# Soft-MoE after soft-capped attention: the last two batches' slot sums on VectorE instead of TensorE, and one filler product less per batch

## The chip, the cores and the metric

The kernel runs on one core of a Trainium2 chip. The metric is the device time of one execution in microseconds (us). Before the change it was 288.38 us, the median of three runs (287.92 to 288.79).

## The reference

Attention over 8 batches, 12 heads, 448 tokens and a head width of 64, with scores capped by tanh, feeds a mixture of experts with soft slots: 3584 tokens of width 768, 8 experts with 4 slots each, so 32 slots.

```
scores = 30 * tanh(q @ k.T / 8 / 30)
attn   = exp(scores - max); attn /= attn.sum(-1)
x      = attn @ v, heads side by side            # 3584 x 768

logits = x @ phi                                 # 3584 x 32
d      = exp(logits); d /= d.sum(0)              # over the tokens
h      = relu((d.T @ x)[e] @ w1[e])              # for each expert e, its 4 slots
slot_out[e] = h @ w2[e]
c      = exp(logits); c /= c.sum(1)              # over the 32 slots of a token
out    = c @ slot_out                            # 3584 x 768
```

The change is about the last softmax: the sum over the 32 slots of each token, by which that token's row of the output is divided.

## The kernel before

All engines' work is issued in one order written out by hand; a list `aux` says which extra job goes into which slot of which step.

**Attention.** A pair is two heads of one batch, with the pair's 448 tokens in 7 tiles of 64 for each head. The 336 tiles are worked off in 56 chunks of six (`CH = 6`), and a batch takes seven chunks (`PER`). In chunk j, ACT takes the tanh of two lots of three score tiles (`tanh_chunk`, L329) and the exponentials of chunk j-1 (`exp_part`, L334), of which DVE does some by a polynomial (L564 to L572). PE forms the scores of the next chunk (`qk_chunk`, L320) into one of two PSUM homes, and the products of the exponentials with V (`pv_mms`, L590). POOL casts V (L287) and issues most of the loads. Each chunk has slots e, a, b, r, c, d, and in slot a of some chunks stand fillers: products of ones into the unused 57 columns of the home of `pv` (`fill`, L620), whose results nobody reads. `FILL` lists them by chunk: (7, 'a', fill, 24) is 24 fillers in slot a of each batch's eighth chunk, between the V products of the first four tiles (`pv_first`) and those of the last 64 query rows (`pv_tail`), ahead of the next `qk_chunk`. It is so in seven batches; for the eighth there is no such chunk.

**Logits, E and the slot inputs.** For each batch PE forms the logits (`logits`, 128 tokens by 32 slots in four groups of tokens, NG = 4, the fourth with 64 rows per half), ACT their exponential `es[b]`, called E (L677, for the last batch L960), and PE the sums E.T @ x (`slot_mms`) over all batches. E has tokens on the partitions and the 32 slots along the free dimension. For the output it is needed turned, with slots on the partitions (`e_transp`): `ET4` for the first six batches, `ETl` for the last two. Batches go in twos: tile c of the batches 2bb and 2bb+1 is one product of 128 tokens.

**The sums.** `e_sums(bb)` (L702 to L706) takes, for one couple of batches, seven products of the turned E with a column of ones (L705) and the reciprocal of the seven sums (L706) into `winv[:, bb, :]`. For the first three couples that stands in the attention part; for the fourth, in the last loop, in front of tile n = 19.

**The tail.** After the last chunk, the last batch's logits and slot sums, then layer 1 of all experts (L1018), relu on ACT and DVE (L1025, L1027), `h_transp` (turns h, L1035, copied by L1039), and layer 2 in two halves of 384 columns (L1046): `for n0 in range(0, 64, 4)` with `layer2(n0, 0)`, then again with half 1. In the first of these loops, at n0 = 16, `h_transp(1)` and `widen(B - 2)` (L1061, DVE: four copies of E side by side, so that one product turns and widens it) are issued. `zdiag`, a float32 tile of 128 x 4 x 32, is used once before that, for the token sums of d (L982, L984).

**Output.** While half 1 of layer 2 runs, the first halves of tiles 0 to 11 are formed (`half_tile`: product L1086, scaling by `winv` on DVE L1088 or ACT L1090, store L1074). Then a loop over n = 0 to 27 forms the second halves of those (n < 12) and both halves of the others (product L1133, scaling L1140 on DVE for odd n, L1142 on ACT for even n). In it, at n = 15 and 17 `e_transp` turns E of the last two batches (L692, L696), and at n = 19 `e_sums(3)` follows. Tiles 21 to 27 are those of the last couple and read `ETl` and `winv[:, 3, :]`. The 11.0 MB of output are stored by SP's queue (L1074), which also reads the spilled part of w2 back before that (L997). The buffers of the output tiles are shared in turn, so a scaling can wait for an earlier store to land.

## Time and profile before

| what | value |
|---|---|
| median of three runs | 288.38 us |
| the profiled execution | 288.24 us |
| its span, first to last instruction | 286.5 us |
| PE busy, products | 250.3 us (87%), 4706 |
| DVE busy | 242.6 us (85%), 502 |
| ACT busy | 254.6 us (89%), 211 |
| POOL busy | 138.9 us (48%), 197 |
| mean granted TensorE clock | 0.981 |
| DMA | 68.11 MB, mean 238 GB/s |

The profile is of one execution; its busy times are shares of a span in which attention, until about 241 us, and the tail have different limits. "Busy" of an engine is time with an instruction on it, so a share near 100% in a stretch says that the engine had no time left there, and the averages over the span do not. In the lists of the timeline, a bracket gives the idle time of that engine before the instruction, and what ended it. PE's weight loads have rows of their own (PEld). A line like L590 is a line of the kernel before.

### The profile page before, as it was taken

How to read it: one execution, taken by the hardware profiler on the slowest of the kernel's cores; microseconds unless marked ns; L12 is line 12 of the kernel's file. 1: busy time of each engine (PE TensorE's matmuls, PEld its weight loads, DVE VectorE, ACT ScalarE, POOL GpSimd, SP SyncE). 2: the span in 40 equal slices, each digit the busy share in tenths (PEclk: the TensorE clock that was granted, in tenths of full speed). 3: DMA queues.
4: the chain of work that ended last, by engine and by line, in shares of the span. 5: the costliest groups of instructions: out<-in, count | busy, mean ns of one | idle time of the engine just before them, and what ended most of it. 6: DMA issues, size and time to landing. Idle time of an engine off the chain costs nothing.

```text
span 286.5 us, 10763 instructions
## 1 busy us (share of the span) xinstructions
PE 250.3 (87%) x4706; PEld 170.3 (59%) x4706; DVE 242.6 (85%) x502; ACT 254.6 (89%) x211; POOL 138.9 (48%) x197
## 2 busy tenths in 40 slices
PE   8888889998999899989998999899899999998710
PEld 7555466756675666566656675667565767642400
DVE  3498999999999999999999999999999986437830
ACT  4999999999999999999999999999999997247720
POOL 7982655664765566555756646574563120200000
PEclk9999999999999999999999999999999999999975
DMA  7999999999999999999999999999999567989995
GB/s 241 257 205 205 201 194 204 224 205 206 232 230 196 209 232 225 217 206 231 227 216 198 226 224 211 214 226 222 206 182 226 137 247 223 409 326 392 414 420 244
DMA packets 58334, 68.11 MB, mean 238 GB/s; under 512 B 4144, under 2 KB 54448, under 8 KB 58288
## 3 DMA queue, kind: packets, MB, share of 16 engines
q0 software_dynamic: 42448, 35.31, 79.1%
q1 hardware_dynamic: 15552, 31.89, 31.7%
q8 instruction: 37, 0.61, 0.8%
q10 hardware_dynamic: 288, 0.23, 0.2%
q14 instruction: 9, 0.07, 0.1%
HBM read 91.72 MB, written 19.27 MB: 387 GB/s over the span
## 4 chain that ended last, share of the span: by engine, by line
DVE 40%; PE 33%; issue 10%; ACT 8%; POOL 5%; DMA 1%; DVEq 0%; ACTq 0%; SPq 0%
PE pv L590 9%; DVE xq L600 7%; PE sc L320 5%; DVE xp L570 4%; DVE xT L652 4%; DVE ex L571 4%; ACT ex L329 4%; DVE xp L568 3%; ACT ex L334 3%; DVE qT L279 3%; POOL vbd L287 2%; DVE ex L564 2%; DVE xp L569 2%; PE so_ps L1046 2%; DVE xf L566 2%
## 5 line engine op out<-in xcount | busy, mean ns | idle before, releaser
L329 ACT ACTIVATE ex<-sc 128x1344 f16<-128x1344 f32 (+1 forms) x113 | 148.3, 1428 | 1.4 <-PE sc L320 1.4
L334 ACT ACTIVATE ex<-ex 128x2688 bf16<-128x2688 f16 (+5 forms) x58 | 115.1, 1993 | 0.1
L590 PE MATMUL pv<-vbd,ex 128*128 128x130 bf16 (+1 forms) x1610 | 95.0, 211 | 11.4 <-POOL vbd L287 8.5
L590 PEld LDWEIGHTS <-ex 128*128 128x128 bf16 (+1 forms) x1680 | 75.7, 101 | 35.9 <-PE sc L320 9.0
L320 PE MATMUL sc<-qT,kT 64*64 64x448 bf16 x672 | 71.4, 360 | 0.5 <-DVE qT L279 0.4
L287 POOL CAST vbd<-vraw 64x896 bf16<-64x896 f32 x46 | 45.9, 998 | 49.5 <-issue 24.5
L600 DVE TENSOR_TENSOR xq<-pv,rec 128x448 bf16<-128x448 f32 x46 | 28.7, 625 | 1.6
L320 PEld LDWEIGHTS <-kT 64*64 64x64 bf16 x672 | 24.1, 105 | 6.3 <-issue 4.0
L295 POOL MEMSET vbd<- 64x1 bf16 x22 | 3.6, 165 | 45.7 <-PE pv L590 45.7
L570 DVE TENSOR_TENSOR xp<-xp,xf 128x1344 f16<-128x1344 f16 (+2 forms) x34 | 25.1, 738 | 0.8
L568 DVE TENSOR_TENSOR xp<-xp,xf 128x1344 f16<-128x1344 f16 (+2 forms) x34 | 25.0, 736 | 0.6
L116 POOL DMA_DIRECT2D w1b<-in_moe_w_dram x32 | 25.3, 792 | 0.0
L571 DVE TENSOR_TENSOR ex<-ex,xp 128x1344 uint16<-128x1344 uint16 (+2 forms) x34 | 24.7, 727 | 0.4
L567 DVE TENSOR_SCALAR xp<-xf 128x1344 f16<-128x1344 uint16 (+2 forms) x34 | 16.8, 494 | 0.4
L184 POOL DMA_DIRECT2D qb<-in_q_dram x22 | 16.7, 757 | 0.5 <-DMA kraw<-in_k_dram 0.5
L279 DVE COPY kT<-kps 128x896 bf16<-128x896 bf16 x23 | 14.2, 617 | 3.0 <-PE kps L274 2.8
L572 DVE TENSOR_SCALAR ex<-ex 128x1344 uint16<-128x1344 uint16 (+2 forms) x34 | 16.5, 485 | 0.1
L277 PEld LDWEIGHTS <-qb 128*64 128x64 bf16 x308 | 10.1, 109 | 10.9 <-issue 10.9
L184 POOL DMA_DIRECT2D kb<-in_k_dram x22 | 16.2, 735 | 0.1
L569 DVE TENSOR_SCALAR xp<-xp 128x1344 f16<-128x1344 f16 (+2 forms) x34 | 15.7, 462 | 0.6
L120 POOL DMA_DIRECT2D w2d<-in_moe_w_dram x21 | 15.9, 777 | 0.4 <-issue 0.4
L620 PE MATMUL pv<-ones 128*128 128x57 bf16 x376 | 16.0, 188 | 0.0
(124 smaller groups left out, 342.1 us busy)
## 6 DMA issues: line engine op xcount, KB each, us to landing
w1b<-in_moe_w_dram POOLq DMA_DIRECT2D x32, 384.0 KB, 9.1
vraw<-in_v_dram SPq DMA_DIRECT2D x44, 224.0 KB, 6.0
w2d<-in_moe_w_dram POOLq DMA_DIRECT2D x21, 384.0 KB, 8.1
w2t<-w2d SPq DMA_DIRECT2D x21, 384.0 KB, 7.1
out_dram<-ob SPq DMA_DIRECT2D x7, 768.0 KB, 8.2
qb<-in_q_dram POOLq DMA_DIRECT2D x22, 224.0 KB, 7.6
kb<-in_k_dram POOLq DMA_DIRECT2D x22, 224.0 KB, 6.1
w2b<-in_moe_w_dram POOLq DMA_DIRECT2D x11, 384.0 KB, 8.1
```

The costliest lines, as they stand in the source:

```text
L116: pool.dma_start(out=w1b[e][:, js, fs], in_=w1r[:, e, js, fs])
L184: pool.dma_start(out=t, in_=quad_ap(nm, Q))
L279: dve.tensor_copy(t, ps)
L287: pool.tensor_copy(vbds[Q % 2][r, :, :, c0:c0 + DH], raw[r])
L320: pe.matmul(sc[cs, u, 0:S], qkT["k", Q][r, c, cs], qkT["q", Q][r, :, cs], start=True, stop=True)
L329: act.activation(exs[j][:, half * CS + u0:half * CS + u1, :].bitcast(F16), (own[0] if i == u0 == 0 else sc)[:, u0:u1, 0:S], ACT.Tanh, scal ...
L334: act.activation(exs[j][:, u0:u1, :], exs[j][:, u0:u1, :].bitcast(F16), ACT.Exp, scale=cap)
L568: lambda: dve.tensor_tensor(p, p, f, op=ALU.mult),
L570: lambda: dve.tensor_tensor(p, p, f, op=ALU.mult),
L571: lambda: dve.tensor_tensor(y, y, p, op=ALU.add),
L590: pe.matmul(out_, exs[j][r, u, q0:q0 + (HP if tail else P)], v_, start=(c == 0 and g == gs[0] < NF), stop=(c == NT - 1), skip_group_check= ...
L600: dve.tensor_tensor(xq[Q][:, h, s0:s1, :], pv[:, 0:s1 - s0, 0:DH], rec.to_broadcast([P, s1 - s0, DH]), op=ALU.mult)
```

## The change

A new function `e_recips(b)` sums E over the 32 slots with one reduction on VectorE, straight from the tokens' layout and for all four groups of a batch at once, into the first columns of `zdiag`; two reciprocals then write the results into `winv`, one for the even and one for the odd tiles, moving them to the batch's half of the partitions. It is issued for the batches B-2 and B-1 behind `widen(B - 2)`, at n0 = 16 of layer 2's first half. `e_sums(3)` at n = 19 goes. And slot a of each batch's eighth chunk has 23 fillers for 24.

```diff
+    def e_recips(b):
+
+        sums = zdiag[:, b % 2, 0:NG]
+        dve.tensor_reduce(sums, es[b], axis=mybir.AxisListType.X, op=ALU.add)
+        to = slice(b % 2 * HP, b % 2 * HP + HP)
+        for odd in range(2):
+            dve.reciprocal(winv[to, b // 2, odd:NT:2],
+                           sums[odd * HP:odd * HP + HP, 0:(NT + 1 - odd) // 2])
...
-    FILL = (..., (7, 'a', fill, 24), (8, 'a', fill, 12), (9, 'a', fill, 4),)
+    FILL = (..., (7, 'a', fill, 23), (8, 'a', fill, 12), (9, 'a', fill, 4),)
...
         if n0 == n2 // 2 - 16:
             h_transp(1)
             widen(B - 2)
+            for b in (B - 2, B - 1):
+                e_recips(b)
         layer2(n0, 0)
...
             e_transp(B - 2)
-        if n == NH + 7:
-            e_sums(B // 2 - 1)
         op = fin.tile([P, 2, 512], F32, name="op", tag="op")
```

In instructions, PE loses seven products and seven weight loads in the last loop, and one filler with its load in seven chunks; DVE loses one reciprocal at tile 19 and gains two reductions and four reciprocals in the first half of layer 2. ACT, POOL and SP have the same instructions in the same order.

More of the change, by code (lines that the diff above doesn't have):

```diff
@@ L749, in spare @@
         busy(n, psV.tile([P, parts * P], F32, name="junk", tag="pv"))
-    FILL = ((4, 'a', fill, 6), (5, 'a', fill, 6), (6, 'a', spare, 3), (6, 'c', spare, 9), (7, 'a', fill, 24), (8, 'a', fill, 12), (9, 'a', fill, 4),)
+    FILL = ((4, 'a', fill, 6), (5, 'a', fill, 6), (6, 'a', spare, 3), (6, 'c', spare, 9), (7, 'a', fill, 23), (8, 'a', fill, 12), (9, 'a', fill, 4),)
     PER = 2 * NQB * NT // CH
```

## The prediction, made before the result was known

> **What bounds the kernel now.** I read the profile from coarse to fine: the slices, then what ACT waited for, then the timeline at the places that the diff touches, then the DMA's rate by windows. On the page, the slices of ACT and of the granted TensorE clock:
> ```profile
> ACT  4999999999999999999999999999999997247720
> ...
> PEclk9999999999999999999999999999999999999975
> ```
> A slice is 7.2 us. ACT is full from the second slice to the 33rd, so for about 230 us the attention part is paced by ACT. The clock stands at nine tenths or more until the last two slices. A 9 may hide a little idle time, so I asked for ACT's waits between 8 and 241 us:
> ```profile
> engine line waited for: us in total, times, longest us
> ACT ex L329 <- PE sc L320: 0.3, 1, 0.3
> ```
> One wait in 233 us, of 0.3 us, and the timeline has it at 31.80 us, ahead of the first of the places where the diff takes a filler out. PE, DVE and POOL have idle time there that costs nothing.

> The first of those places in the timeline (start, us, engine, line, operation; in brackets the idle time before it):
> ```profile
> 35.32 2.46 ACT L329 ACTIVATE ex<-sc 128x1344 f16<-128x1344 f32 x2
> ...
> 35.78 0.34 PE L590 MATMUL pv<-vbd,ex 128*128 128x130 bf16 x3 [0.45 <-DVE ex L572]
> ...
> 35.96 0.80 PE L620 MATMUL pv<-ones 128*128 128x57 bf16 x24
> ...
> 36.84 0.54 PE L320 MATMUL sc<-qT,kT 64*64 64x448 bf16 x4
> ...
> 37.66 2.08 ACT L334 ACTIVATE ex<-ex 128x2240 bf16<-128x2240 f16 x1
> ...
> 39.62 2.48 ACT L329 ACTIVATE ex<-sc 128x1344 f16<-128x1344 f32 x2
> ...
> 40.06 0.84 PE L590 MATMUL pv<-vbd,ex 128*128 128x130 bf16 x12 [0.91 <-POOL vbd L287]
> ```
> The 24 fillers (L620) stand ahead of the next score products (L320). Those end at 36.84 + 0.54 = 37.38, and ACT takes them up at 39.62, when it is done with the exponentials: 2.24 us of lead. In the other six batches I find the same pattern with 2.2 to 2.5 us.

> After 241 us the end is in two parts. First PE alone (layer 1, layer 2, the first output products) until 255; then the stores. The windows (us of the span; busy us of PE, PEld, DVE, ACT, POOL; clock, DMA share, GB/s):
> ```profile
> 255.00:260.00 5.00, 5.00 (x59) 1.37 (x58) 2.79 (x5) 3.56 (x7) 0.00 (x0) 1.00 0.78 292
> ...
> 270.00:275.00 5.00, 2.56 (x13) 1.03 (x11) 3.19 (x4) 3.39 (x4) 0.00 (x0) 1.00 1.02 421
> 275.00:280.00 5.00, 0.00 (x0) 0.00 (x0) 0.79 (x1) 0.00 (x0) 0.00 (x0) 0.58 1.01 418
> 280.00:286.50 6.50, 0.00 (x0) 0.00 (x0) 0.00 (x0) 0.00 (x0) 0.00 (x0) 0.50 0.54 223
> ```
> The last computation ends inside 275:280, and the DMA moves 418 GB/s x 5 us + 223 x 6.5 = 3.5 MB after 275: a third of the output's 11.0 MB. All the engines are done and the stores still run for some 8 us. So the end is the time of the first store plus the bytes at the DMA's rate.

> **The change, part by part.** *One filler less, in seven batches* (PE, attention). Six fillers take 0.32 us (at 53.16), 24 take 0.80: (0.80 - 0.32) / 18 = 0.027 us each, 0.19 us for seven. It hides behind the lead of 2.2 us, and the PE time it frees runs into the next wait (0.91 us on POOL above). I take 0. If that cover were gone, the gain would be 0.19 at most, all seven on the path; a loss is possible only through the clock (a rival below).

> *Added on DVE: two reductions and four reciprocals*, emitted behind the second widening copy (L1061). The rows of the tail:
> ```profile
> 245.97 0.29 DVE L984 TENSOR_REDUCE zacc<-zdiag 128x1 f32<-128x128 f32 x1
> 246.29 0.16 DVE L985 RECIPROCAL rz<-zacc 128x1 f32<-128x1 f32 x1
> ...
> 252.26 0.28 DVE L1061 COPY so<-E 128x512 bf16<-128x512 bf16 x1
> ...
> 255.04 0.58 ACT L1090 ACTIVATE obh<-op,winv 128x384 f32<-128x384 f32 x1 [0.42 <-PE op L1086]
> ...
> 255.26 0.62 DVE L1088 TENSOR_SCALAR obh<-op,winv 128x384 f32<-128x384 f32 x1 [2.71 <-PE op L1086]
> 255.64 0.34 SPq L1074 DMA_DIRECT2D out_dram<-obh  x1
> ```
> A reduction of 128x128 takes 0.29; a reciprocal 0.16 for one column, 0.18 for four (L597 at 241.50), 0.20 for seven. The new ones read 128x128 as four rows of 32 and write four and three columns. So 2 x (0.29 + 2 x 0.18) = 1.30 us, and six gaps of 0.03 as between L984 and L985 give 1.48: from 252.54 to 254.02. Behind them on DVE waits the scaling at 255.26, which now waits for PE anyway: 1.24 us are left of its 2.71. ACT's first scaling reads the same tile of weights at 255.04 and may now have to wait for the last of them: 1.02 us are left. No shape of the reduction stands in the trace as it will run. Bounds: 0.16 for each of the six from below (0.96 us, ends 253.5), and the widest DVE row near it, 0.62 for 128x448 (L600), for each reduction with 0.36 (L600, 128x192) for each reciprocal from above, 2 x 0.62 + 4 x 0.36 + 0.18 = 2.86, ends 255.40. That is 0.36 late for ACT's first scaling, 0.14 for DVE's. I take 0, since the 128x128 row has the same element count; bounds 0 to +0.36.

> [...]

> *Taken out of the tail*: seven products with their weight loads, the reciprocal, and the wait between them.
> ```profile
> 268.12 0.32 PE L705 MATMUL wps<-ones,ETl 128*128 128x1 bf16 x7
> ...
> 268.37 0.90 ACT L1142 ACTIVATE ob<-op,winv 128x768 f32<-128x768 f32 x1 [0.62 <-DMA out_dram<-obh]
> 268.62 0.20 DVE L706 RECIPROCAL winv<-wps 128x7 f32<-128x7 f32 x1
> ```
> PE gets back 0.32 us and DVE 0.20. At that very place ACT waits for a store to land and free its buffer: the DMA, not the arithmetic, lets the tiles through. What is late next is the DMA queue. The last store is issued at 276.0 and takes 9.6 us to land, where the quickest of the small ones takes 2.5; computation could end some 6 us sooner or later and the bytes would still be the last. I take 0. If the cover were gone, 0.32 + 0.20 = 0.52 us would be gained. No DMA is added, dropped or moved, and neither SP's nor POOL's queue is passed by anything.

> **Sum.** 0 + 0 + 0. The profiled execution took 288.24 us: 286.5 of span and 1.7 around it. The runs' median is 288.38, from 287.92 to 288.79. I predict 288.2, the profiled time to the tenth; 0.3% is 0.87 us, about what a measurement of this kernel can tell from no change.

> **Rivals.**
> 1. *The tail is not bound by the DMA.* For it: in 255:260 the share is 0.78, and the half-tile stores land in 2.5 us, so nothing queues for long there. Against: from 260 on the share is 1.0, and the last part removed lies at 268. It would give 288.24 - 0.52 = 287.7, with the fillers' 0.19 on top 287.5.
> 2. *The new DVE work holds the first output tiles.* Place: ACT's first scaling at 255.04, ahead of the first store, which sets when the DMA starts. It decides once the six take more than 2.50 us, 0.42 each on average; at the upper bound 288.24 + 0.36 = 288.6. Slower than noise it is only from 3.4 us on. Against: no small DVE row comes near this.
> 3. *The clock falls for want of fillers* (slower). Place: the stretch behind the shortened run, where PE is least busy (3.71 of 5 us in 35:40). In 275:280 the clock's mean is 0.58: it goes to 0.50 at about 275.8, 1.9 us after the last product ended at 273.97. So an idle stretch of some length halves it. At half speed, one cycle of about 4.2 us of ACT (233 us over 56 chunks), with some 3.8 us of PE work, would put PE back by 3.8 us; less its lead of 2.24 and 0.4 of idle time, ACT would wait 1.2 us. Once is 289.4, in all seven batches 296.6. Against: the longest idle time of PE that I find between 20 and 240 us is 0.91 us, and the clock stood; a filler less makes it 0.94. It decides only if the gate sits between the two.

> [...]

> That the change does not do what it says I give nothing: counted in the program, PE has 14 products and 14 loads less, DVE six instructions for one.

> **How the numbers follow.** Forecast (nothing shows) 0.74, around 288.2 with the scatter of the runs, 0.45 to each side. Rival 1 0.10, mostly within the bound: 0.04 of it beyond, with fillers and scatter. Rival 2 0.04, a quarter beyond. Rival 3 0.06, all beyond. 0.06 for what no view shows (code that lies elsewhere in memory, another chip), two thirds beyond the bound, split evenly with rounding. Faster 0.04 + 0.03 = 0.07; slower 0.01 + 0.06 + 0.03 = 0.10; same 0.83. The range reaches down to rival 1 with fillers and scatter, 287.5 - 0.2 = 287.3, and up to rival 2's bound with scatter, 288.6 + 0.5 = 289.1; rival 3 stays outside.

> **What would show it.** ACT in attention: its waits between 8 and 241 us stay at about 0.3, and the last exponential ends at the same time. Clock: 1.00 in all windows to 275. DVE: the six end before 254.3, and the scalings at 255.04 and 255.26 still wait for PE. Tail: the last scaling may end up to 0.5 us sooner than 275.8, but the first store goes out at the same time and the DMA's share stays 1.0 from 260, so the span stays at 286.5. I am wrong if the span moves with the last scaling (the DMA had room), if ACT waits for scores at the filler (no cover), or if the first store moves.

## The result, and the profile after

The changed kernel took 287.44 us (median of 22 runs, 286.03 to 288.31), the kernel before 288.08 in runs beside it (22, 287.31 to 289.05): a ratio of 0.9972, 95% interval 0.9960 to 0.9983. That is 0.28% less: below the 0.3% that I had called what can be told from no change, but with that many runs clear of zero. I had forecast that nothing shows; the time itself lies inside the range that I gave. The profiled execution took 287.43 us, with a span of 285.1 for 286.5; so 2.3 us lie around the span for 1.7, and the span shows more of a gain than the time.

Attention is as it was. The page's slices of ACT and of the granted clock, and ACT's waits between 8 and 241 us, after the change:
```profile
ACT  4999999999999999999999999999999998237730
...
PEclk9999999999999999999999999999999999999985
```
```profile
ACT ex L329 <- PE sc L320: 0.3, 1, 0.3
```
The last exponential ends at 240.96 us for 241.12, and the first tanh had already begun 0.10 sooner. The new DVE work in the timeline (start, us, operation, idle time ahead of it):
```profile
252.10 0.28 DVE L1070 COPY so<-E 128x512 bf16<-128x512 bf16 x1
252.30 0.28 DVE L711 TENSOR_REDUCE zdiag<-E 128x4 f32<-128x128 bf16 x1
252.61 0.35 DVE L714 RECIPROCAL winv<-zdiag 64x4 f32<-64x4 f32 x2
252.98 0.29 DVE L711 TENSOR_REDUCE zdiag<-E 128x4 f32<-128x128 bf16 x1
253.30 0.36 DVE L714 RECIPROCAL winv<-zdiag 64x4 f32<-64x4 f32 x2
255.11 0.62 DVE L1097 TENSOR_SCALAR obh<-op,winv 128x384 f32<-128x384 f32 x1 [1.45 <-PE op L1095]
```
The six end at 253.66, and the scaling behind them still waits 1.45 us for PE. The first store is issued at 255.48 for 255.64, the last scaling ends at 275.63 for 275.79: 0.16 sooner, no more than the first store. The last two scalings on DVE, before and after:
```profile
273.85 1.94 DVE L1140 TENSOR_SCALAR ob<-op,winv 128x768 f32<-128x768 f32 x2 [1.38 <-PE op L1133]
```
```profile
273.69 1.94 DVE L1149 TENSOR_SCALAR ob<-op,winv 128x768 f32<-128x768 f32 x2 [1.40 <-PE op L1142]
```

So up to the end of the computation the two executions differ by 0.16 us. The rest of the 1.4 us lies in the stores. The windows of the changed kernel (the columns as in the prediction):
```profile
255.00:260.00 5.00, 4.89 (x58) 1.30 (x58) 2.96 (x6) 3.59 (x7) 0.00 (x0) 1.00 0.79 295
270.00:275.00 5.00, 2.40 (x12) 0.93 (x10) 3.35 (x4) 3.22 (x4) 0.00 (x0) 1.00 1.00 419
275.00:280.00 5.00, 0.00 (x0) 0.00 (x0) 0.63 (x1) 0.00 (x0) 0.00 (x0) 0.56 1.03 429
280.00:285.10 5.10, 0.00 (x0) 0.00 (x0) 0.00 (x0) 0.00 (x0) 0.00 (x0) 0.50 0.62 255
```
From the first store's first packet to the last packet's end it is 256.32 to 283.62, 27.30 us; before, 256.49 to 285.11, 28.62. The DMA queues between 257 and 284 us show what else was on the engines, first before, then after (queue: packets, MB, share of 16 engines; stores: count, KB, us from issue to landing):
```profile
q1 hardware_dynamic: 4539, 10.81, 101.2%
q8 instruction: 1, 0.02, 0.2%
...
out_dram<-ob SPq DMA_DIRECT2D x7, 768.0 KB, 8.2
```
```profile
q1 hardware_dynamic: 4490, 10.76, 100.5%
...
out_dram<-ob SPq DMA_DIRECT2D x7, 768.0 KB, 7.0
```
Queue q8 carries instructions, by its kind on the page: one packet of 16 KB in the middle of the stores before, none after. The median of the seven large stores lands 1.2 us sooner after its issue; in the span, the stores that land behind the packet are 1.4 to 1.8 us sooner, and the two just ahead of it 0.3 to 0.4. In the trace's packets the one of before starts at 272.6 us and takes 0.947 us. The page of the kernel before has the whole queue:
```profile
q8 instruction: 37, 0.61, 0.8%
```
These 37 packets come 256 PE instructions apart on average (9212 records between the first and the last, over 36), so I take q8 as what loads PE's code; I call the place at which a packet is due an edge. Single gaps run from 122 to 388 records in this kernel, so an edge can't be placed to the record by counting. The packet at 272.6 came 11 PE records ahead of PE's last; the changed kernel's PE has 28 instructions less (9384 products and loads for 9412), and no packet comes while the stores run: the next is at 286.7, when everything is done.

That gives **theory F** (code loading): a block of PE's code fetched among the stores holds one of 16 full DMA engines, whose share of the last stores ends late. **Rivals**: T, the products and the wait taken out of the last loop make the end sooner; C, the fillers held attention up. All three are consistent with the changed kernel alone.

### The profile page after: what moved, and what is told of

Same layout as the page of the kernel before. It is cut to its first block, busy times and chain, and to the rows that moved or that the text cites. A ratio compares the mean times of both kernels' runs of the same rounds, so it can differ in the third digit from the quotient of the medians.

```text
span 285.1 us, 10742 instructions
## 1 busy us (share of the span) xinstructions
PE 249.9 (88%) x4692; PEld 169.8 (60%) x4692; DVE 243.6 (85%) x507; ACT 254.5 (89%) x211; POOL 139.4 (49%) x197
## 4 chain that ended last, share of the span: by engine, by line
DVE 43%; PE 30%; issue 10%; ACT 6%; POOL 6%; DMA 1%; DVEq 0%; ACTq 0%; SPq 0%
PE pv L590 9%; DVE xq L600 7%; PE sc L320 5%; DVE ex L571 4%; DVE xp L570 4%; DVE xT L652 4%; DVE xp L568 3%; POOL vbd L287 3%; DVE qT L279 3%; DVE ex L564 2%; ACT ex L334 2%; DVE xf L566 2%; PE junk L835 2%; DVE xp L569 2%; PE so_ps L1055 2%
## 5 line engine op out<-in xcount | busy, mean ns | idle before, releaser
L329 ACT ACTIVATE ex<-sc 128x1344 f16<-128x1344 f32 (+1 forms) x113 | 149.8, 1454 | 1.4 <-PE sc L320 1.4
L334 ACT ACTIVATE ex<-ex 128x2688 bf16<-128x2688 f16 (+5 forms) x58 | 116.8, 2027 | 0.1
L590 PE MATMUL pv<-vbd,ex 128*128 128x130 bf16 (+1 forms) x1610 | 95.2, 211 | 11.3 <-POOL vbd L287 8.4
L590 PEld LDWEIGHTS <-ex 128*128 128x128 bf16 (+1 forms) x1680 | 75.7, 101 | 36.0 <-PE sc L320 8.9
L320 PE MATMUL sc<-qT,kT 64*64 64x448 bf16 x672 | 71.5, 360 | 0.6 <-DVE qT L279 0.4
L287 POOL CAST vbd<-vraw 64x896 bf16<-64x896 f32 x46 | 46.3, 1006 | 48.9 <-issue 23.9
L600 DVE TENSOR_TENSOR xq<-pv,rec 128x448 bf16<-128x448 f32 x46 | 28.7, 624 | 1.6
L320 PEld LDWEIGHTS <-kT 64*64 64x64 bf16 x672 | 24.2, 105 | 6.4 <-issue 4.2
L572 DVE TENSOR_SCALAR ex<-ex 128x1344 uint16<-128x1344 uint16 (+2 forms) x34 | 16.4, 484 | 0.1
L620 PE MATMUL pv<-ones 128*128 128x57 bf16 x369 | 15.8, 188 | 0.0
L652 DVE COPY xT<-xps 128x896 bf16<-128x896 bf16 (+1 forms) x24 | 14.3, 597 | 1.7 <-PE xps L643 1.7
```

Of the source, the lines that this page charges most:

```text
L287: pool.tensor_copy(vbds[Q % 2][r, :, :, c0:c0 + DH], raw[r])
L320: pe.matmul(sc[cs, u, 0:S], qkT["k", Q][r, c, cs], qkT["q", Q][r, :, cs], start=True, stop=True)
L329: act.activation(exs[j][:, half * CS + u0:half * CS + u1, :].bitcast(F16), (own[0] if i == u0 == 0 else sc)[:, u0:u1, 0:S], ACT.Tanh, scal ...
L334: act.activation(exs[j][:, u0:u1, :], exs[j][:, u0:u1, :].bitcast(F16), ACT.Exp, scale=cap)
L590: pe.matmul(out_, exs[j][r, u, q0:q0 + (HP if tail else P)], v_, start=(c == 0 and g == gs[0] < NF), stop=(c == NT - 1), skip_group_check= ...
L600: dve.tensor_tensor(xq[Q][:, h, s0:s1, :], pv[:, 0:s1 - s0, 0:DH], rec.to_broadcast([P, s1 - s0, DH]), op=ALU.mult)
```

## The experiments

Ratios are to the kernel before, run on the same chip in the same five rounds, 11 or 12 runs of each kernel beside 35 of the kernel before (the second line: 22 and 22). The four kernels from "fill only" to "14 products at the end" ran on one chip, the eight below them on another. "Stores" is the time from the first store's first packet to the last packet's end, in the profiled execution. "Block" is when a block of PE's code was fetched between 257 and 284 us.

| kernel | PE instructions against before | block at, us | stores, us | ratio (95%) |
|---|---|---|---|---|
| before | 0 | 272.6 | 28.62 | 1 |
| changed | -28 | none | 27.30 | 0.9972 (0.9960 to 0.9983) |
| fill only | -14 | 273.0 | 28.61 | 0.9998 (0.9982 to 1.0013) |
| sums only | -14 | 273.0 | 29.22 | 1.0008 (0.9996 to 1.0020) |
| instructions back | 0 | 268.4 | 28.51 | 1.0006 (0.9991 to 1.0021) |
| 14 products at the end | 0 | 275.1 | 28.89 | 0.9993 (0.9980 to 1.0006) |
| changed, again | -28 | none | 27.58 | 0.9975 (0.9957 to 0.9992) |
| 20 fillers | -70 | none | 28.54 | 0.9978 (0.9962 to 0.9995) |
| 22 fillers only | -28 | none | 28.13 | 0.9990 (0.9971 to 1.0010) |
| 142 products at the end | +256 | 274.5 | 28.71 | 0.9991 (0.9976 to 1.0007) |
| same count, 7 at the end | -28 | none | 27.34 | 0.9981 (0.9962 to 1.0001) |
| other filler | -28 | none | 27.54 | 0.9978 (0.9959 to 0.9998) |
| half a block | +42 | 264.8 | 28.64 | 0.9994 (0.9977 to 1.0012) |
| a whole block | +224 | none | 27.74 | 1.0033 (1.0015 to 1.0051) |

### The two parts alone

Fill only:
```diff
-    FILL = (..., (7, 'a', fill, 24), ...)     # the kernel before
+    FILL = (..., (7, 'a', fill, 23), ...)
```

> The kernel before with 23 fillers for 24 and nothing else: PE has 14 instructions fewer (7 products, 7 loads). Theory F (code loading): PE's code comes in blocks of 16 KB; in the kernel before, one block is fetched at 272.6 us, 11 PE records ahead of its last, by one of 16 DMA engines that are full of stores, and that engine ends late; 14 instructions fewer push the fetch past PE's end. F expects a ratio of about 0.997 (0.996 to 0.998), the profile without a block fetch between 256 and 284 us; if 14 are not quite enough, a fetch at 273 to 276 and no gain. Theory T (the products and the wait taken out of the last loop make the end sooner): 1.000, since they are all still there. Theory C (the fillers held up attention): 0.997, with the last exponential some 0.8 us sooner.

Sums only:
```diff
-    FILL = (..., (7, 'a', fill, 23), ...)     # the changed kernel
+    FILL = (..., (7, 'a', fill, 24), ...)
```

> The changed kernel with 24 fillers again: only the slot sums go to VectorE. PE has 14 instructions fewer than before (7 products, 7 loads in the last loop). Theory F: as with the fillers alone, 0.997 (0.996 to 0.998), no block fetch between 256 and 284 us. Theory T: 0.997, and the computation of the last tile ends 0.5 to 0.8 us sooner. Theory C: 1.000.

Neither part moves the time by itself: 0.9998 and 1.0008. So it is not the sum of two gains, and T and C both fall in the form in which one part would carry the effect. F had to take its second branch: 14 instructions fewer were not enough, and the block still came among the stores, at 273.0 us in both. By the count of 11 records in the kernel before, 14 should have been enough; the single gaps of 122 to 388 records say how little such a count can promise. The DMA queues of "fill only" between 257 and 284 us:
```profile
q8 instruction: 1, 0.02, 0.2%
...
out_dram<-ob SPq DMA_DIRECT2D x7, 768.0 KB, 8.1
```
Its large stores land as in the kernel before. In "sums only" the stores took 29.22 us, the most of all, and the last packet ended at 285.23 us for 285.11: its first store began 0.48 us sooner than in the kernel before, and its second was held up in a way that comes up again below. This branch was written down ahead, but it could hardly have failed: what tells more is putting instructions back.

### Instructions put back

In attention, with the slot sums left on VectorE:
```diff
-    FILL = (..., (9, 'a', fill, 4),)     # the changed kernel
+    FILL = (..., (9, 'a', fill, 6),)
```

> The changed kernel with six fillers for four in slot a of each batch's tenth chunk: 14 products and 14 loads more in attention, so that PE has as many instructions as in the kernel before; the slot sums stay on VectorE. Theory F: the block is again fetched in the store stage, at about 272 us, and the gain is gone: ratio 1.000 (0.999 to 1.001), time at the last tile's computation unchanged, the last store 0.9 us later than in the changed kernel. Theory T: 0.997, as the changed kernel. Theory C: 1.000 or above, with the last exponential later by up to 0.4 us.

Behind PE's last output product, where PE is idle:
```diff
+    ps = psT.tile([P, P], F32, name="pad_ps", tag="T")     # the changed kernel
+    for _ in range(14):
+        pe.matmul(ps, ones, ones, start=True, stop=True)
```

> The changed kernel with 14 products and loads of ones behind PE's last output product, where PE has nothing else to do; nobody reads them. Attention, fillers and the last loop are those of the changed kernel. Theory F: PE crosses the block's edge at about 274 us, the fetch falls into the store stage (3.5 MB still to go after 275), and the gain is gone: ratio 1.000 (0.999 to 1.001). Theories T and C: 0.997, as the changed kernel.

Both lose the gain (1.0006 and 0.9993). The second tells most, as attention and the last loop are those of the changed kernel. Its last scaling ends at 275.62 us, as in the changed kernel (275.63), and its 14 products are over by 274.6; yet the DMA ends at 285.21 for 283.62. The queues between 257 and 284:
```profile
q8 instruction: 1, 0.02, 0.2%
...
out_dram<-ob SPq DMA_DIRECT2D x7, 768.0 KB, 8.6
```
T falls: nothing of what it names was put back. In the packets, each store ends with sixteen writes of four bytes. I take them as one for each of the 16 DMA engines; the packets do not name their engine. In the changed kernel, fifteen of the last store's come at about 283.2 us and one 0.4 later. In this one, all but one such straggler come together until the block; for the first store that ends after it, fourteen at 276.01, the straggler 0.4 later, and one 1.74 later, at 277.75. From there on every store has one write that late: fourteen of the last store's come at 283.46, and one at 285.20. I read them as one engine, which falls back at the block and never catches up. Of the 1.6 us by which the DMA ends later than in the changed kernel, this lag makes 1.3; by the other 0.25 all engines end later. Work on an idle engine thus cost 1.3 us of this profile, by my reading by way of the code that it made PE load. All six kernels with a block between 264 and 276 us, and the kernel before, have such a write 1.5 to 1.8 us behind; in those without one the last write is 0.4 to 0.9 us behind.

### The changed kernel again, and three more that move the edges

The changed kernel beside these three:

> The changed kernel itself, on the chip of the next three. All theories: 0.997 (0.996 to 0.9985). Theory F (code loading): no PE block fetch between 256 and 284 us, and the 16 DMA engines end within 0.5 us of each other; with fetch, one ended 1.7 to 1.8 us behind the first thirteen.

It repeats: 0.9975, and no block among the stores; the engines end within 0.8 us, for the 0.5 that I expected, fourteen of them together.

20 fillers, to bring the block ahead of it into the stores:
```diff
-    FILL = (..., (7, 'a', fill, 23), ...)     # the changed kernel
+    FILL = (..., (7, 'a', fill, 20), ...)
```

> The changed kernel with 20 fillers for 23: 42 PE instructions fewer than the changed kernel, so that the block now fetched at 254.7 us, in the pause between the last weights and the first stores, moves to about 256.7, behind the first stores. Theory F: it costs again, ratio 0.998 to 1.000, one DMA engine late from 257 us on. Theory C (fillers held up attention): at most 0.997, as the changed kernel or faster. Theory T (the products taken out of the last loop): 0.997, as the changed kernel.

A miss for F. The block came at 256.0 us, but no engine is late: all 16 end within 0.4 us of each other. The stores took 28.54 us in the profile, for another reason, of which more below; the time is 0.9978, below what I expected and that of the changed kernel within the interval, so the runs show no loss.

22 fillers only, with the slot sums on PE as before:
```diff
-    FILL = (..., (7, 'a', fill, 24), ...)     # the kernel before
+    FILL = (..., (7, 'a', fill, 22), ...)
```

> The kernel before with 22 fillers for 24 and nothing else: as many PE instructions as in the changed kernel, but the slot sums stay on PE in the last loop. Theory F: 0.997 (0.996 to 0.9985), no block fetch between 256 and 284 us. Theory T: 1.000. Theory C: twice the effect of one filler less, which showed none (0.9998): 1.000.

Inconclusive by its time (0.9990, which takes in 1 as well as 0.9975). The profile has no block among the stores and all engines ending within 0.4 us, as F says; but the stores took 28.13 us. Its first stores show why. First the second store's issue on SP in this kernel, then in the changed one:
```profile
255.68 1.29 SPq L1074 DMA_DIRECT2D out_dram<-obh  x1
```
```profile
255.91 0.38 SPq L1083 DMA_DIRECT2D out_dram<-obh  x1
```
The block ahead of the last one was fetched here at 255.7 us, for 254.7 in the changed kernel, and SP's issue beside it took 0.9 us longer. The windows 256 to 258 and 258 to 260 have
```profile
256.00:258.00 2.00, 2.00 (x25) 0.56 (x21) 1.50 (x3) 1.26 (x3) 0.00 (x0) 1.00 0.54 200
258.00:260.00 2.00, 1.76 (x21) 0.56 (x21) 0.75 (x3) 1.62 (x3) 0.00 (x0) 1.00 1.05 390
```
The changed kernel moves 326 GB/s in the first of them for these 200, so all stores behind the first begin late. The kernel with 20 fillers has the same with its third store (1.33 us for 0.40, the block at 256.0). Five more kernels have it with the second store, whose issue takes 0.38 us otherwise: sums only 1.05 us, other filler 0.68, 14 products at the end 0.66, 142 products 0.50, instructions back 0.49. In these five and in the kernel with 22 fillers only, the issue began while the block's packet was on its way and ended 0.36 to 0.38 us behind the packet's end, as if it had waited for it. The first store's issue did not wait: in "fill only" and "other filler" it took its usual 0.34 us beside a packet. So with a block beside the first stores the store stage is longer too (28.13 and 28.54 us for 27.30); that it costs time is not shown, as 0.9978 and 0.9990 are the ratios of the two kernels that have most of it with no block behind.

Two blocks at the end:
```diff
+    ps = psT.tile([P, P], F32, name="pad_ps", tag="T")     # the changed kernel
+    for _ in range(14 + 128):
+        pe.matmul(ps[:, 0:57], ones, ones[:, 0:57], start=True, stop=True)
```

> The changed kernel with 142 idle products and loads (57 columns) behind PE's last output product: 284 instructions more, so two blocks' edges in the store stage for none, at about 275 and 278 us. Theory F: two fetches of 0.95 us on the same DMA engine; the late engine ends about 2.7 us behind the first thirteen, for 1.7 to 1.8 with one; ratio 1.001 to 1.004. Theories T and C: 0.997, as the changed kernel, since PE has nothing to do there.

A miss. Only one block was fetched among the stores (274.5 us); the gain went as with one (0.9991, the last engine 1.7 us behind most others). Behind its packet PE has 177 records left, fewer than the 256 between two packets on average, so the second was not due by that count. That a second costs as much again is not shown.

### Count against place

Same count as the changed kernel, 14 instructions moved from attention to the end:
```diff
-    FILL = (..., (7, 'a', fill, 23), ...)     # the changed kernel
+    FILL = (..., (7, 'a', fill, 22), ...)
...
+    ps = psT.tile([P, P], F32, name="pad_ps", tag="T")
+    for _ in range(7):
+        pe.matmul(ps, ones, ones, start=True, stop=True)
```

> The changed kernel with 22 fillers for 23 and seven idle products and loads behind PE's last output product: as many PE instructions as the changed kernel, 14 of them moved from attention to the end. Theory F (a PE code block fetched in the store stage): no fetch there from 257 us on, 0.9975 (0.996 to 0.999), where 14 idle products at the end without taking any out gave 0.9993; the block before it, at 254.7 us in the changed kernel, moves to about 255.3. Rival P (idle products at the end cost something by themselves): 0.9985 or above with the 16 DMA engines ending together. Theory T (the last loop): 0.9975.

The filler taken from another place:
```diff
-    FILL = (..., (7, 'a', fill, 23), (8, 'a', fill, 12), ...)     # the changed kernel
+    FILL = (..., (7, 'a', fill, 24), (8, 'a', fill, 11), ...)
```

> The changed kernel with 24 fillers again in the eighth chunk's slot a and 11 for 12 in the ninth's: as many PE instructions as the changed kernel, the filler taken from another place. Theory F: 0.9975 (0.996 to 0.999), no fetch from 257 us on. Theory C in its weaker form (it matters that slot a of the eighth chunk has 23): 1.000, as with the slot sums alone (1.0008).

0.9981 and 0.9978: both as the changed kernel. Seven idle products at the end show no cost while no block falls among the stores; the queues of "same count" between 257 and 284 us:
```profile
q1 hardware_dynamic: 4587, 10.88, 101.7%
...
out_dram<-ob SPq DMA_DIRECT2D x7, 768.0 KB, 7.1
```
And which of the two fillers goes does not matter. That the eighth chunk has 23 is not what counts.

Half a block and a whole one:
```diff
-    FILL = (..., (9, 'a', fill, 4),)     # the changed kernel
+    FILL = (..., (9, 'a', fill, 9),)     # half a block; a whole one: 22
```

> The changed kernel with nine fillers for four in slot a of each batch's tenth chunk: 70 PE instructions more than the changed kernel, 42 more than before. Theory F: the last block's edge moves forward into the middle of the stores, a fetch at about 260 to 266 us, one DMA engine at least 0.9 us behind the others at the end, ratio 0.999 to 1.001. Theory C: 1.000 or above, growing with the fillers, so above what 126 more of them would give only if fewer. Theory T: 0.9975.

> The changed kernel with 22 fillers for four in slot a of each batch's tenth chunk: 252 PE instructions more, almost a whole block of 256, so that the edges fall where they fall in the changed kernel, four instructions later. Theory F: as the changed kernel, 0.9975 (0.996 to 0.999), no fetch from 257 us on, though PE does 126 products more. Theory C (fillers hold attention up): above the kernel with nine fillers, 1.001 or more.

Half a block is as F says: the block at 264.8 us, ratio 0.9994, the last engine 1.6 us behind most others. The whole block is half a hit. No block among the stores, and the stores took 27.74 us, as in the changed kernel; but the time is 1.0033. There C is right: from the end of the first tanh to that of the last exponential it is 235.88 us for 233.84 in the changed kernel, and ACT's waits before 243 us grow to
```profile
ACT ex L329 <- PE sc L320: 0.9, 3, 0.3
ACT E L677 <- PE lps L661: 0.2, 1, 0.2
```
18 fillers more in a slot of tenth chunks lengthen attention by 2 us; five more (half a block, 233.68 us) did not, and one less in the eighth chunk did not shorten the time (fill only, 0.9998). ACT's waits account for only half of the 2 us; where the rest lies stays open.

Taken together: the six kernels with a block at 264 to 276 us stand at 0.9991 to 1.0008, the six without one at 0.9972 to 0.9990, the whole block with its longer attention apart. Each of the six intervals with a block takes in 1; of those without, four leave it out, and those of "22 fillers only" and "same count" do not. The means are 0.9998 and 0.9979, so the block costs about 0.2%, 0.55 us; in the profiles the stores take 28.5 to 29.2 us with it and 27.3 to 28.5 without. The changed kernel stands twice among the six without, and its first ratio is what the search began with. Without it, and on one chip alone, "142 products" and "half a block" stand at 287.91 us on average (24 runs), and "20 fillers", "22 fillers only", "same count" and "other filler" at 287.53 (48 runs): 0.38 us apart, with a 95% interval of 0.11 to 0.64 from resampling the runs.

## Why the prediction was wrong

- **The fillers**, taken at 0: right. Alone they gave 0.9998, and ACT's one wait stayed 0.3 us. The lead that was to cover them is 2.0 to 2.1 us in the other six batches, by the ends of the score products, and not 2.2 to 2.5; nothing hung on that.
- **The new DVE work**, taken at 1.48 us and hidden: right. It took 1.28 us (252.38 to 253.66), and 1.45 of the 2.71 us of idle time were left, for 1.24 predicted.
- **The work taken out of the tail**, taken at 0 because the DMA sets the end: right. The last scaling moved by as much as the first store (0.16), and with the sums alone the time was 1.0008. Rival 1, with a time near the measured one (287.7), had the cause wrong: the tail is bound by the DMA (the last packet ends 9.3 us behind the last scaling, for my "some 8"), and I take that as why the fetch is seen at all. That 287.44 lies inside my range is luck: the range reached that low only for this rival.
- **"No DMA is added, dropped or moved"**: this is the step that failed. It holds for the DMAs that the kernel issues. PE's own code comes over a DMA queue too, by my reading of q8: here 37 packets of 16 KB, one for 256 instructions on average; and the change takes 28 instructions out ahead of an edge that was met 11 PE records before PE's end. I had the row: the page's queue list has q8 with 37 packets, and I left it out. Code that lies elsewhere shared 0.06 of my chances with another chip, as something "no view shows"; the DMA queues by window show this fetch.
- **"I take 0"** for the sum was thus short by a term of -0.55 us, the mean difference of the kernels with and without the block; the changed kernel itself gained 0.64 by the medians.
- **The clock** stood (1.00 in the windows up to 275 us), and with 20 fillers too (1.00 from 20 to 275): rival 3 did not come. It fell to 0.50 only at 275.62 us, 1.81 behind the end of PE's last product, where before it was 275.84 us and 1.87; at what shorter idle time it falls, no run shows. Neither did rival 2: the first scalings on DVE and ACT still waited for PE.

The traces give a block's size, 16384 bytes in each of the kernel before's 37 packets, and 256 records from one to the next on average. For the block that fell among the stores, with the DMA's share at 1.01 to 1.07 from 260 to 280 us, the runs show a cost, 0.55 us; what the other 36 cost no run shows.

What stays open: the block's packet takes 0.95 us, but the late write falls back by about 1.5 to 1.8 behind most others; what fills the rest no view shows. Why SP's issue of a store beside a packet takes longer, up to 1.33 us for 0.40, is not shown either. One or two writes are 0.4 to 0.9 us late with and without a block (one 1.2 in "142 products"), and why is not known. The profiles' stores differ by 1.3 us between the two kernels, the times by 0.64 of the median; part of that is the time around the span, 2.3 us for 1.7 in the profiled execution. The only kernel without a block that keeps the sums on PE is "22 fillers only", whose time is inconclusive; that the count alone gives the whole gain there too rests on its profile, in which no engine is late. And whether the block ahead of the last costs in the changed kernel in some of its runs, when it comes a little later than 254.7 us, was not tried.

## What to carry to other kernels

When a kernel ends in a stretch where all DMA engines are full, count the code of its engines among the transfers: look for the instruction queues' packets in that stretch (here one of PE's, 16 KB and 0.95 us, at 272.6 us). How far the last instruction is from an edge could not be counted to the record here, with gaps of 122 to 388 records; idle instructions added at the end showed it (14 brought a block among the stores), and so did some taken out (28 less, and none came). An edit of a few instructions that moves no work was worth some 0.2% here, lost with 14 idle products at the end (0.9993 for 0.9972), and the effect belongs to the count and not to the edit; so before a small gain is put down to the edit, pad it back to the old count. Here neither half of the change moved the time by itself, and both together took the block out of the stores.
